# Twelve products of the identity with itself behind two of the prologue's weight transposes

## The chip, the cores and the metric

The kernel runs on one core of a Trainium2 chip. A core has five engines that work side by side, each on its own stream of instructions in order: TensorE (PE; its weight loads, PEld, are listed apart), VectorE (DVE), ScalarE (ACT), GpSimd (POOL) and SyncE (SP), which here only issues transfers. The metric is the device time of one execution in microseconds. TensorE's clock has two levels, 1.2 and 2.4 GHz; the profile gives the granted clock of a stretch as a share of the higher one.

## The reference

Attention with 8 heads over 8 batches of 576 tokens (head size 64), then a normalised feed-forward layer (512 to 2048 to 512) with a residual:

```python
scores = scale * np.matmul(q, k.transpose(0, 1, 3, 2))
mask_local = (rel >= 0) & (rel < 32)                       # heads 0 to 3
mask_strided = (rel >= 0) & (pos[None, :] % 32 == pos[:, None] % 32)   # heads 4 to 7
scores = np.where(masks, scores, -1e9)
attn = softmax(scores)                    # with 1e-9 added to the sum
x = np.matmul(attn, v)                    # heads side by side: 512 columns
xn = (x - mean(x)) / np.sqrt(var(x) + 1e-06) * g_ln
out = x + np.maximum(xn @ w_ch1, 0.0) @ w_ch2
```

All inputs and the output are float32.

## The kernel before

The 8 x 576 tokens are worked on as nine chunks of 512. The feed-forward weights lie in 16 blocks of 128 hidden columns, and each value is split into a high and a low part, so that a product is made of three. From about 45 us to the end TensorE runs these products almost without a gap, and the attention of later batches lies between them.

The **prologue** ahead of that (the first 45 us, and thinner until about 85 us) fills the pipeline. It prepares two batches of attention and the first eight weight blocks. Heads go in pairs: a, b, c, d are the four pairs of batch 0, and a1 to d1 those of batch 1. Pairs a and c are local, b and d strided; the names in the trace end in 0, 2, 1, 3 for a, b, c, d. The order of the prologue is written out by hand in the table `ORDER`, as steps with a letter and a pair (or a weight block):

- `L`: load; `R`: bring the two heads of a pair side by side (a copy `flat` by POOL or DVE, L371); `T`: nine transposes on TensorE (`t` and `tr`, L377); `C`: copies of the turned queries and keys (`qt`, `kt`, L388 to L396).
- `S`: scores (`sp`, L445 local, L457 strided); `M`: add the mask (`sm`, L472); `Z`, `U`, `E`: maximum, subtraction, exponential.
- `P`: transposes of the attention weights (`pp`, L498: five of 128 columns for a local pair, six for a strided one); `G`: ACT's copy of them (`pt`, L503); `V`: the product with the values (`av`, L514 or L523); `O`: divide by the sums (`xo`); `X`: transposes of the output (`px`, L559); `H`, `Y`: its high and low parts (`xh`, `xl`).
- `w0.cm` and the like: steps of weight block 0. `cm` (L270) is a float32 product 128 wide that gives a column mean.
- `F1`: the first products of the feed-forward layer, for chunk 0 (`ph`, L970).

Each engine takes its instructions in the order in which the steps were written; the end of the kernel ties every instruction to the one ahead of it on its engine. A step on TensorE that waits therefore holds up all later steps on TensorE. Loads are issued by SP in order too, and a rule in the loop over the steps lets each wait until earlier loads have landed, so that only so many are under way.

PSUM, into which TensorE writes, is shared out as banks. In the prologue the pool `ps_x` holds a working bank and two tiles, `s0` and `s1`, that the first products of the weight blocks 0 and 1 use (step `F1`, `product`). At its start the program runs four products of the identity with itself (`idle`, L922), 512 columns wide.

Of the kernel before, what the change touches and what calls it, by code (L numbers as in the profile page):

```python
# [8 lines left out]
F32 = mybir.dt.float32  # L9
# [10 lines left out]
ORDER = """  # L20
L.a L.b L.c R.a/DVE L.X0 T.a L.Y0 R.b/POOL C.ka/ACT C.qa/DVE L.X1 T.b R.c/POOL S.a L.d C.qb/DVE
C.kb/ACT M.a w0.sc0 T.c w0.lo0 Z.a/DVE S.b C.qc/ACT L.va w0.mg0 U.a C.kc/ACT w0.sg0 M.b S.c
w0.lo1 w0.bg w0.sc1 Z.b/DVE E.a w0.mg1 U.b w1.sc0 L.vb P.a w0.sg1 M.c R.d/POOL w1.lo0 E.b w1.mg0
w0.cs T.d G.a w1.sg0 P.b w1.bg C.qd/DVE C.kd/ACT L.Y1 L.vc G.b Z.c/DVE w0.cm S.d w0.ce U.c V.a
M.d L.X2 w0.hi0 w1.cs O.a E.c V.b L.Y2 w0.lw0 O.b w1.sc1 X.a w1.cm H.a L.a1 Z.d/DVE w1.lo1 X.b
D.c/POOL Y.a H.b w1.mg1 P.c L.vd Y.b G.c U.d w2.sc0 w1.sg1 w0.hi1 V.c w1.ce E.d w0.lw1 F1.0.b
O.c w2.lo0 P.d L.b1 w2.sc1 w2.mg0 R.a1/POOL G.d X.c w2.sg0 H.c T.a1 w2.lo1 w2.bg Y.c L.X3 w2.mg1
L.va1 C.ka1/ACT V.d w2.cs w2.sg1 F1.0.a C.qa1/ACT O.d w2.hi1 S.a1 L.Y3 w1.hi0 R.b1/POOL X.d M.a1
L.c1 w1.lw0 H.d Z.a1/DVE T.b1 w3.lo0 U.a1 Y.d F1.1.b w3.sc0 F1.1.a C.qb1/ACT C.kb1/DVE D.a1/POOL
# [17 lines left out]
def kernel(  # L47
# [10 lines left out]
    nc = tc.nc  # L58

    B, H, S, D = q.shape  # L60
    DM, DFF = w1.shape
    P = 128
# [9 lines left out]
    CH = 512  # L72
# [25 lines left out]
    ps_x = sums_ctx.enter_context(  # L98
        tc.tile_pool(name="ps_x", bufs=1, space=bass.MemoryType.PSUM, side="right"))
# [11 lines left out]
    ident = keep.tile([P, P], F32, name="ident")  # L111
# [731 lines left out]
    def ffn2(run, f, h, tiles):  # L843
        for i in tiles:
            products(run.po[i], f, h, i, slice(0, DM), f == run.f0, f == run.f1 - 1)
# [135 lines left out]
    def second(n, half):  # L981
        if n == "0" and not half:
            sums_late()
            runs[0].open()
            banks[:] = [(ps_a, "a")]
        x = hidden[int(n)]
        ffn2(runs[0], int(n), (x["h"], x["l"]), range(2 * half, 2 * half + 2))

    weights = {"sc": Split.scaled, "lo": Split.low, "mg": Split.magnitude, "sg": Split.sign,
               "bg": Split.by_g, "cs": Split.chunks_sum, "cm": Split.column_mean,  # L990
               "ce": Split.centred, "hi": Split.high, "lw": Split.rest}
# [8 lines left out]
        "V": lambda x: named[x].v_values(), "O": lambda x: named[x].v_scale(),  # L1000
        "St": lambda x: named[x].x_store(), "X": lambda x: named[x].x_rows(),
        "H": lambda x: named[x].x_high(), "Y": lambda x: named[x].x_low(),
        "F1": product, "hh": high, "hl": low,
        "F2a": lambda n: second(n, 0), "F2b": lambda n: second(n, 1)}
    FLIGHT = 45
    queued = []
# [12 lines left out]
    for step in ORDER.split():  # L1019
        what, x = step.split(".", 1)  # L1020
        n0 = len(tc.nc.cur_bb.bb.instructions)
        if what[0] == "w":
            i = x[2:]
# [3 lines left out]
        for ins in tc.nc.cur_bb.bb.instructions[n0:]:  # L1027
            if "DMA" not in type(ins).__name__:
                continue
            n, behind = len(queued), 0  # L1030
# [396 lines left out]
    for i, x in enumerate(residuals):  # L1427
        po = fresh_bank(f"po{B}_{i}")
        n = NFC if i + 1 < NT else NFC - 2
# [54 lines left out]
```

## Time and profile before

| what | value |
|---|---|
| three timed runs | 895.68, 898.46, 900.03 us; median 898.46 us |
| the profiled execution | 896.8 us, of it the span of the profile 895.0 us |
| TensorE busy | 878.1 us, 98% of the span |
| DVE, ACT, POOL busy | 455.5, 242.2, 238.7 us |
| mean granted clock | 0.994 |
| TensorE busy in the first 45 us | 33.49 us |

Times within the profile count from the span's start. "Idle" is the time in which an engine ran nothing just ahead of an instruction, and the profile names what ended it. A "record" is what TensorE shows of an instruction: a float32 product makes two, a transpose one.

### The profile page before, as it was taken

To read this page: it belongs to the slowest core of one execution; us is meant where nothing else is said; L and a number is where in the kernel's file an instruction comes from. 1 tells how busy PE (TensorE), PEld (TensorE's weight loads), DVE (VectorE), ACT (ScalarE), POOL (GpSimd) and SP (SyncE) were. 2 spreads that over 40 slices of the span, in tenths; PEclk is the share of its full clock that TensorE was granted. 3 is DMA by queue.
4 is the path that set the end of the run, shared out by engine and by line. 5 is a ranking of instruction groups with operands and counts; after the bars stand their busy time and mean duration, and the time that the engine had idled before them with its cause. 6 is when DMAs were issued, how large, how long until landed. Compare 5 with 4: busy or idle time off the path is not lost.

```text
span 895.0 us, 18342 instructions
## 1 busy us (share of the span) xinstructions
PE 878.1 (98%) x7431; PEld 721.1 (81%) x7431; DVE 455.5 (51%) x855; ACT 242.2 (27%) x433; POOL 238.7 (27%) x293
## 2 busy tenths in 40 slices
PE   6899999999999999999999999999999999999998
PEld 4678888888888888888888888888888788888886
DVE  5797475446745455544645455455652764232400
ACT  4666465112211111111111111112122443333200
POOL 6678187110100010000100000001000468676000
PEclk9899999999999999999999999999999999999999
DMA  9999881117786655756585759596942001001210
GB/s 210 205 212 254 199 259 36 21 46 176 149 166 117 119 106 107 143 113 117 97 150 103 133 96 171 107 134 130 167 109 79 13 13 47 1 0 44 91 32 23
DMA packets 330972, 100.64 MB, mean 112 GB/s; under 512 B 269712, under 2 KB 321800, under 8 KB 330888
## 3 DMA queue, kind: packets, MB, share of 16 engines
q1 hardware_dynamic: 259320, 86.41, 43.7%
q10 hardware_dynamic: 71568, 13.07, 9.8%
q8 instruction: 58, 0.95, 0.5%
q14 instruction: 26, 0.21, 0.1%
HBM read 72.37 MB, written 27.06 MB: 111 GB/s over the span
## 4 chain that ended last, share of the span: by engine, by line
PE 95%; ACT 1%; DVE 1%; DMA 1%; issue 1%; SPq 0%; POOL 0%; POOLq 0%; ACTq 0%
PE po L840 44%; PE ph L815 33%; PE u L1250 5%; PE sv L659 5%; PE v L1250 2%; PE c L1250 1%; PE px L690 1%; DMA rows<-in_k_dram 1%; PE pp L498 1%; PE av L514 0%; PE cm L270 0%; PE t L377 0%; PE ph L970 0%; PE px L559 0%; PE sp L457 0%
## 5 line engine op out<-in xcount | busy, mean ns | idle before, releaser
L840 PE MATMUL po<-w,hh 128*128 128x512 f32 x1024 | 320.4, 394 | 0.0
L815 PE MATMUL ph<-xh,w 128*128 128x512 f32 x880 | 290.4, 391 | 0.0
L840 PEld LDWEIGHTS po<-w,hh 128*128 128x128 f32 x1024 | 188.9, 188 | 39.3
L826 DVE SCALAR_TENSOR_TENSOR hl<-ph,hh 128x512 fp32r<-128x512 f32 x112 | 77.4, 691 | 268.9 <-ACT hh L821 268.9
L840 PE MATMUL po<-w,hl 128*128 128x512 f32 x512 | 199.4, 390 | 0.0
L815 PEld LDWEIGHTS ph<-xh,w 128*128 128x128 f32 x880 | 165.2, 188 | 34.2
L815 PE MATMUL ph<-xl,w 128*128 128x512 f32 x440 | 171.2, 389 | 0.0
L821 ACT ACTIVATE hh<-ph 128x512 fp32r<-128x512 f32 x112 | 66.9, 597 | 339.8 <-PE ph L815 258.7
L488 POOL TENSOR_TENSOR sm<-sm,mx 128x640 f32<-128x640 f32 (+1 forms) x32 | 40.6, 1269 | 344.9 <-issue 201.1
L840 PEld LDWEIGHTS po<-w,hl 128*128 128x128 f32 x512 | 96.1, 188 | 20.5
L815 PEld LDWEIGHTS ph<-xl,w 128*128 128x128 f32 x440 | 82.7, 188 | 16.8
L493 ACT ACTIVATE sm<-sm 128x640 f32<-128x640 f32 (+1 forms) x32 | 23.8, 742 | 104.3 <-POOL sm L488 104.3
L782 POOL TENSOR_TENSOR rs<-rs,mhalf 128x1 f32<-128x1 f32 x28 | 15.4, 551 | 121.3 <-DVE rs L781 93.1
L840 PE MATMUL po<-w,h 128*128 128x512 f32 x186 | 42.3, 389 | 0.0
L1117 POOL TENSOR_TENSOR sr<-sr,w 128x256 f32<-128x256 f32 x48 | 40.2, 837 | 3.8
L840 PEld LDWEIGHTS po<-w,h 128*128 128x128 f32 x186 | 34.9, 188 | 7.2
L1117 POOL TENSOR_TENSOR s<-sr,s 128x256 fp32r<-128x256 f32 x32 | 24.7, 803 | 25.5 <-ACT s L1236 25.5
L239 DVE SCALAR_TENSOR_TENSOR p<-s,p 128x512 uint32<-128x512 uint32 x32 | 22.0, 688 | 11.4 <-ACT p L235 11.2
L484 DVE TENSOR_REDUCE mx<-sm 128x10 f32<-128x640 f32 (+1 forms) x32 | 26.3, 822 | 1.9
L1117 DVE TENSOR_TENSOR x<-po,x 128x512 f32<-128x512 f32 x8 | 5.3, 688 | 39.6 <-PE po L840 29.9
L671 DVE TENSOR_TENSOR xo<-sv,den 128x256 f32<-128x256 f32 (+1 forms) x72 | 24.0, 389 | 0.0
L1117 DVE TENSOR_TENSOR p<-u,p 128x512 f32<-128x512 f32 x8 | 5.5, 692 | 34.1 <-PE u L1250 34.1
(193 smaller groups left out, 995.6 us busy)
## 6 DMA issues: line engine op xcount, KB each, us to landing
s<-in_moe_w_ch_dram SPq DMA_DIRECT2D x32, 512.0 KB
out_dram<-x SPq DMA_DIRECT2D x32, 256.0 KB
raw<-in_q_dram SPq DMA_DIRECT2D x104, 72.0 KB
raw<-in_k_dram ACTq DMA_DIRECT2D x68, 72.0 KB
x<-xdl SPq DMA_DIRECT2D x34, 128.0 KB
x<-xds SPq DMA_DIRECT2D x34, 128.0 KB
xdl<-xo SPq DMA_DIRECT2D x16, 256.0 KB
wd<-sm SPq DMA_DIRECT2D x10, 384.0 KB
```

The lines of the kernel that those rows point to most:

```text
L239: nc.vector.scalar_tensor_tensor(out=self.p[i], in0=self.bits(i), scalar=3, in1=self.p[i], op0=ALU.logical_shift_left, op1=ALU.bitwise_or)
L484: engine(self.mx[:, :, 0:nt], self.smv, axis=AX.X)
L488: nc.gpsimd.tensor_tensor(out=sm, in0=sm, in1=mx[:, :, 0:nt].unsqueeze(3).broadcast_to([P, 2, nt, w]), op=ALU.subtract)
L493: nc.scalar.activation(out=self.smv, in_=self.smv, func=AF.Exp, scale=SCALE)
L659: nc.tensor.matmul(dst, at, by, start=True, stop=True, tile_position=pos)
L671: nc.vector.tensor_tensor(out=xot[0:n, :, t0:t1], in0=src, in1=pv.den[0:n, :, t0:t1].unsqueeze(3).broadcast_to([n, 2, t1 - t0, D]), op=ALU ...
L815: nc.tensor.matmul(ph, w[:, cc], x[:, cc, :], start=(n + k == 0), stop=(n == NCC - 1 and k == 2))
L821: nc.scalar.activation(out=hh, in_=ph, func=AF.Relu)
L826: nc.vector.scalar_tensor_tensor(out=hl, in0=ph, scalar=0.0, in1=hh.bitcast(F32), op0=ALU.max, op1=ALU.subtract)
L840: nc.tensor.matmul(po, hx[:, cs], w, start=(start and n == 0), stop=(stop and n == 2))
L1117: engine.tensor_tensor(out=out, in0=a, in1=b, op=op)
L1250: nc.tensor.matmul(po, a[:, c], b[:, c, :], start=(start and c + k == 0), stop=(stop and c == 1 and k == 2), skip_group_check=True)
```

## The change

A new kind of step, `K`, stands in the table twice: `K.8` right behind `P.a`, and `K.4` right behind `P.c`. It multiplies the 128 x 128 identity by itself in float32, eight and four times, into the first 128 columns of a PSUM tile with the tag `s1`. Nothing reads the result, and the tile's place is used by `F1` later.

```diff
-w0.lo1 w0.bg w0.sc1 Z.b/DVE E.a w0.mg1 U.b w1.sc0 L.vb P.a w0.sg1 M.c R.d/POOL w1.lo0 E.b w1.mg0
+w0.lo1 w0.bg w0.sc1 Z.b/DVE E.a w0.mg1 U.b w1.sc0 L.vb P.a K.8 w0.sg1 M.c R.d/POOL w1.lo0 E.b w1.mg0
...
-D.c/POOL Y.a H.b w1.mg1 P.c L.vd Y.b G.c U.d w2.sc0 w1.sg1 w0.hi1 V.c w1.ce E.d w0.lw1 F1.0.b
+D.c/POOL Y.a H.b w1.mg1 P.c K.4 L.vd Y.b G.c U.d w2.sc0 w1.sg1 w0.hi1 V.c w1.ce E.d w0.lw1 F1.0.b
...
+    def beats(n):
+        t = ps_x.tile([P, CH], F32, tag="s1", name=f"beats{n}")[:, 0:P]
+        for i in range(int(n)):
+            nc.tensor.matmul(t, ident, ident, start=True, stop=True)
...
-        "F1": product, "hh": high, "hl": low,
+        "K": beats, "F1": product, "hh": high, "hl": low,
```

On TensorE the first place reads as follows before the change, from pair c's scores (`sp_1`) over pair a's weight transposes (`pp_0`) and pair d's transposes (`t_3`, `tr_3`) to pair d's scores (`sp_3`); the numbers behind are those of the tiles:

```order
L445 MATMUL sp_1_381<-kt_l,qt_l 32x64 x36
L498 MATMUL pp_0_435<-ident,sm_200 128x128 x5
L377 MATMUL t_3_454<-ident,flat_3_446 128x128 x8
L377 MATMUL tr_3_455<-ident,flat_3_446 128x128
L498 MATMUL pp_2_469<-ident,sm_199 128x128 x6
L270 MATMUL cm_490<-r_0_377,mean 128x128
L457 MATMUL sp_3_492<-kt_s,qt_s 64x54 x22
```

And after it, in the same place on TensorE:

```order
L445 MATMUL sp_1_381<-kt_l,qt_l 32x64 x36
L498 MATMUL pp_0_435<-ident,sm_200 128x128 x5
L992 MATMUL beats_441<-ident 128x128 x8
L377 MATMUL t_3_463<-ident,flat_3_455 128x128 x8
L377 MATMUL tr_3_464<-ident,flat_3_455 128x128
L498 MATMUL pp_2_478<-ident,sm_199 128x128 x6
L270 MATMUL cm_499<-r_0_377,mean 128x128
L457 MATMUL sp_3_501<-kt_s,qt_s 64x54 x22
```

Eight products stand between pair a's weight transposes and pair d's transposes; the rest is in its old order, with other tile numbers.

The second place on TensorE before the change, from the second column mean over pair c's weight transposes (`pp_1`) and its product with the values (`av_1`) to the first products of weight block 0:

```order
L270 MATMUL cm_611<-r_1_467,mean 128x128
L559 MATMUL px_2_623<-ident,xo_2_603 128x128 x6
L498 MATMUL pp_1_636<-ident,sm_200 128x128 x5
L514 MATMUL av_1_658<-v_l_188,pt_1_650 32x65 x40
L970 MATMUL ph_0_702<-xh_613,w_0_562 128x512
```

And after it:

```order
L270 MATMUL cm_620<-r_1_476,mean 128x128
L559 MATMUL px_2_632<-ident,xo_2_612 128x128 x6
L498 MATMUL pp_1_645<-ident,sm_200 128x128 x5
L992 MATMUL beats_651<-ident 128x128 x4
L514 MATMUL av_1_672<-v_l_188,pt_1_664 32x65 x40
L970 MATMUL ph_0_716<-xh_622,w_0_571 128x512
```

Four products stand between pair c's weight transposes and its product with the values. The other engines and SP's loads keep their order throughout. The added products wait for nothing but their turn on TensorE.

## Rows read from the trace of the kernel before

**Rows 1.** The page: TensorE's granted clock in tenths, 40 equal slices.

```profile
PEclk9899999999999999999999999999999999999999
```

**Rows 2.** Stretches (us): busy time and instructions by engine, clock, DMA share, GB/s.

```profile
17.50:20.00 2.50, 0.94 (x6) 0.63 (x6) 2.46 (x6) 1.96 (x4) 1.47 (x2) 0.97 1.04 180
20.00:25.00 5.00, 3.76 (x16) 3.39 (x17) 2.47 (x5) 1.89 (x5) 3.37 (x5) 0.50 1.01 182
25.00:27.50 2.50, 2.50 (x116) 2.22 (x116) 1.19 (x2) 1.52 (x4) 2.42 (x4) 0.66 1.31 196
27.50:30.00 2.50, 2.04 (x88) 1.79 (x70) 2.31 (x8) 0.62 (x2) 2.38 (x3) 1.00 1.10 315
30.00:32.50 2.50, 1.62 (x13) 1.18 (x12) 2.48 (x4) 2.07 (x4) 1.80 (x2) 1.00 1.01 244
32.50:35.00 2.50, 1.29 (x81) 1.12 (x80) 2.30 (x4) 2.43 (x6) 0.64 (x2) 0.71 0.66 131
35.00:37.50 2.50, 2.50 (x32) 1.93 (x16) 2.00 (x5) 1.28 (x3) 1.97 (x2) 0.61 0.61 147
45.00:100.00 55.00, 54.28 (x646) 43.90 (x645) 40.50 (x70) 32.40 (x57) 36.52 (x36) 1.00 0.90 214
```

**Rows 3.** Timeline of TensorE: start, duration (us), instruction, records [idle before, releaser].

```profile
17.94 0.77 PE L498 MATMUL pp<-ident,sm 128*128 128x128 f32 x5
21.01 1.97 PE L377 MATMUL t<-ident,flat 128*128 128x128 f32 x8 [2.31 <-DVE r L245]
...
24.70 0.77 PE L270 MATMUL cm<-r,mean 128*128 128x128 f32 x2 [0.23 <-ACT kt_s L396]
25.40 1.49 PE L457 MATMUL sp<-kt_s,qt_s 64*64 64x54 f32 x44
...
29.83 0.39 PE L270 MATMUL cm<-r,mean 128*128 128x128 f32 x2
30.69 0.84 PE L559 MATMUL px<-ident,xo 128*128 128x128 f32 x6 [0.48 <-DVE xo L539]
31.93 0.77 PE L498 MATMUL pp<-ident,sm 128*128 128x128 f32 x5 [0.40 <-DVE xl L604]
33.91 1.41 PE L514 MATMUL av<-v_l,pt 64*32 64x65 f32 x80 [1.21 <-ACT pt L503]
```

**Rows 4.** Timeline of TensorE's weight loads at the program's start.

```profile
3.23 0.34 PEld L922 LDWEIGHTS idle<-ident 128*128 128x128 f32 x1 [0.52 <-issue]
```

**Rows 5.** Timeline of TensorE where the granted clock is 1.00.

```profile
14.14 0.91 PE L457 MATMUL sp<-kt_s,qt_s 64*64 64x54 f32 x44
...
43.63 1.06 PE L377 MATMUL t<-ident,flat 128*128 128x128 f32 x8 [0.26 <-DVE sm L478]
...
47.05 1.26 PE L457 MATMUL sp<-kt_s,qt_s 64*64 64x54 f32 x44 [0.17 <-DVE kt_s L396]
...
50.06 1.04 PE L514 MATMUL av<-v_l,pt 64*32 64x65 f32 x80
```

**Rows 6.** Chain of work that ended last: start, duration (us), what.

```profile
35.32 1.58 PE ph L970 x3
...
40.78 0.89 PE ph L970 x3
```

**Rows 7.** Timelines of POOL, DVE and ACT, around the two places.

```profile
19.81 1.14 POOL L371 COPY flat<-rows 128x1152 f32<-128x1152 f32 x1 [1.01 <-DMA rows<-in_k_dram]
...
20.27 0.69 DVE L245 SCALAR_TENSOR_TENSOR r<-s,p 128x512 uint32<-128x512 uint32 x1
...
32.70 1.11 DVE L604 TENSOR_TENSOR xl<-px,xh 128x480 fp32r<-128x480 f32 x2 [0.22 <-ACT xh L599]
...
24.27 0.28 ACT L396 COPY kt_s<-tr 128x64 f32<-128x64 f32 x1
```

**Rows 8.** POOL's copy of b1; SP's waits from 26 to 42 us (total, times, longest).

```profile
41.84 1.15 POOL L371 COPY flat<-rows 128x1152 f32<-128x1152 f32 x1 [1.37 <-DMA rows<-in_k_dram]
...
SPq L419 <- DMA s<-in_moe_w_ch_dram: 2.9, 2, 2.3
```

## The prediction

> **What bounds the kernel now.** I read the clock line of the page first [rows 1]: TensorE is granted its full clock in every slice of 22 us but the second (about 22 to 45 us), which shows 8 tenths. The program is bound by TensorE (878.1 us of the 895.0 us span are busy, the table above), so what can be won at all is idle time or slow time in the prologue. The stretch table places it [rows 2]: the mean clock is 0.97 from 17.5 to 20 us, 0.50 from 20 to 25 us, 0.66 from 25 to 27.5 us, 1.00 until 32.5 us, then 0.71 and 0.61. There are only two levels, 1.2 and 2.4 GHz, so 0.97 means that half clock began 0.15 us before 20 us, and 0.66 that it ended 1.7 us after 25 us: about 19.85 to 26.7 us. The second spell is 1.45 us of one stretch and 1.95 us of the next: 33.55 to 36.95 us. That is 10.2 us at half clock, and since half clock can cost no more than half of the time spent in it, 5.1 us is the ceiling of everything that this change can win by the clock: 0.57% of 896.8 us.
>
> What came before each fall: from 17.5 to 20 us TensorE was busy 0.94 of 2.50 us, from 30 to 32.5 us 1.62 of 2.50 us. From 27.5 to 30 us it was busy 2.04 us and the clock stayed [rows 2]. The timeline shows the two holes [rows 3]: the first pair's weight transposes end at 18.71 us and the next work, pair d's transposes, starts at 21.01 us; the third pair's end at 32.70 us and the next, its values product, starts at 33.91 us. The change puts work into just these two holes.
>
> **Part 1, the eight products behind the first pair.** Price: a float32 product 128 wide makes two records on TensorE. The nearest row is the column mean (same shape and type): 0.39 us a product at full clock, 0.77 us at half [rows 3]. That includes the end of the pipe, so eight of them cost at most 3.1 us at full clock. For a stream I take the four products at the program's start: their records are 512 wide and the weight loads start 0.86 us apart (0.34 us busy behind 0.52 us of idle time) [rows 4]. A quarter of the width is 0.21 us a record. I read this as the pace at half clock, though the page's first slice shows 9 tenths or more [rows 1], since eight transposes 128 wide take 1.06 us at full clock and 1.97 us at half, some 0.11 and 0.21 us apart once the last one's end is off [rows 3, 5]. So 16 records take 15 x 0.107 + 0.28 for the last (0.39 less 0.107) = 1.9 us at full clock, 3.4 to 3.7 us at half. I take 1.9 us. They start behind the fifth transpose, at about 18.5 us, and end at 20.4 us (21.6 us by the column mean's price).
>
> Is that hidden? The queue behind them holds pair d's transposes. These wait for POOL's copy, which ends at 20.95 us, and start at 21.01 us; the row names a DVE operation that ends at 20.96 us [rows 3, 7]. So there is 0.55 us of cover; by the upper price the delay is 0.6 us. The destination is a PSUM tile that nobody reads, and the order shows no wait on the products, so no other engine gets a new wait.
>
> What they change: TensorE is busy from 17.8 to 20.4 us instead of 18.7. From 17.5 to 20 us it is then busy for 0.94 + 1.29 = 2.2 us, much as in the stretch from 27.5 us (2.04 us), behind which the clock stayed [rows 2]. I take it that the clock holds here too. Then pair d's transposes take 1.06 us instead of 1.97 (0.91 less), the column mean 0.39 instead of 0.77 (0.38 less), and the strided scores 0.91 instead of 1.49 (0.58 less) [rows 3, 5]. Pair b's six transposes between are covered by the wait for ACT's copy that ends at 24.55 us [rows 3, 7]; that copy follows pair d's transposes through DVE, so it comes 0.91 us earlier. Sum: 1.87 us earlier at the first values product. The DVE chain from there to 32 us follows TensorE step by step, so I carry 1.87 us on to the third pair.
>
> A page speaks on the rest of this stretch. Of the 1.62 us before the second fall nearly all was transposes (six of pair b's output, 0.84 us, five of pair c's weights, 0.77 us) [rows 2, 3], and yet the clock fell. The Trainium skill, "TensorE: Matmul & The Clock Gate", section "Part 4: PE-mode transpose", says that transposes do not count as busy time for the clock; this trace agrees at that fall. By that rule real products, as here, are the right filler, but the transposes of pairs d and b behind them hold nothing; what that would give is the second rival.
>
> **Part 2, the four products behind the third pair.** Eight records: 7 x 0.107 + 0.28 = 1.0 us at full clock, 1.6 us by the single price, 1.9 us at half. They start about 32.5 us and end at 33.5 us. The values product behind them starts at 33.91 us because it needs the ACT copy and a PSUM bank that DVE reads until 33.81 us [rows 3, 7]: 0.4 us of cover, and a delay of 0.2 to 0.5 us by the other prices. If the second spell goes, the values product takes 1.04 instead of 1.41 us (0.37) [rows 3, 5], and the three products behind it 0.89 instead of 1.58 us on the chain (0.69) [rows 6]: 1.06 us. Both parts together: 2.93 us at most.
>
> **What is late next.** This does not all arrive. Pair b1's transposes start at 43.63 us [rows 5]. They need POOL's copy of b1's rows, which starts at 41.84 us after 1.37 us of waiting for a load, and lasts 1.15 us [rows 8]: it ends at 42.99 us. SP issues that load in order behind the values' loads, whose waits are for other loads (2.9 us, the longest 2.3 us) [rows 8], not for TensorE. So it will land where it did, and with 0.05 us to react the transposes cannot start before 43.05 us: 0.58 us earlier, not 2.93. TensorE works in order, so everything behind them waits too. After that 0.17 us of idle time is left to win, at the scores of 47.05 us, which wait for DVE's copy of the same transposes [rows 5]; from 45 us on TensorE is busy 54.28 of 55 us [rows 2]. Sum: 0.58 + 0.17 = 0.75 us. The ends: 0.2 us, if the upper prices of both parts eat the gain before the load, and 1.2 us, if the load lands half a microsecond earlier.
>
> The profiled execution took 896.8 us (span 895.0); the sum on it is 896.05 us. The three timed runs are 895.68, 898.46 and 900.03 us, so it lies below their median; the mean of all four is 897.74 us, and I set the cases against that: 897.74 - 0.75 = **897.0 us**.
>
> **The rivals.**
> - The full gain arrives: the load of b1 lands earlier in most executions, and 2.93 us come through: 894.8 us. For it: nothing in one trace says how far a load's landing moves from run to run. Against it: in this trace POOL waits 1.37 us for it [rows 8].
> - The clock falls later, not less: the 15 transposes of pairs d and b follow the eight products and the clock drops behind them. Then 0.91 us of part 1 stays, but two values products run at half clock (0.37 us each), and 0.17 us is left; if the second spell stays as well, that is all: 897.6 us. For it: 1.62 us of transposes did not hold the clock from 30 us [rows 2].
> - Slower: the added products run at half clock. If the clock has fallen by 18.5 us instead of 19.85 us, the eight end at about 22.0 us and hold up pair d by 1.0 us; the four end 0.4 us after the values product could start. All of it is on TensorE's path: 1.4 us, 899.1 us. It decides from a fall 1.35 us earlier than here. Against it: the clock is 0.97 in the whole stretch [rows 2].
> - The change does nothing: identity products leave the clock as it is and are hidden: 897.7 us.
>
> **How the numbers follow.** Forecast 0.50, full gain 0.16, later fall 0.16, slower 0.12, nothing 0.06. The four times shown differ by 4.35 us with the same code, so a median of three moves by a good microsecond either way. From 894.0 (the full gain, with 0.7 us of that) to 899.6 us (the slower case with 0.5 us) I leave out about 2 in 10. Half a per cent, 4.5 us, is about what a measurement of this kernel can tell from no change: faster means under 893.97, slower over 902.95. Only the full gain with a low run reaches the first (0.05), and only the slower case with two high runs the second (0.03).
>
> **What the profile after would show.** Right: clock 1.00 from 17.5 to 27.5 us and from 32.5 to 37.5 us; the products done by 20.4 and near 32 us; pair d's transposes in about 1.06 us; POOL's copy of b1 still near 41.8 us, after a longer wait, with TensorE idle in front of b1's transposes, which start near 43.05 us. Wrong: a copy of b1 that starts well before 41 us (full gain); half clock between 22 and 30 us (later fall); products 0.21 us apart with pair d's transposes behind 21.5 us (slower). A change of over 4 us in either direction would show that something outside the prologue moved.

## The result and the profile after

The changed kernel takes 901.55 us (median of 11 runs, 899.17 to 906.36), the kernel before 897.3 us in the same comparison (11 runs, 895.68 to 900.03). The ratio is 1.0051, with a 95% interval from 1.0031 to 1.0070: slower by 2.8 to 6.3 us, and outside the range that was forecast. (A ratio here is that of the whole comparison, not the quotient of the two medians.) The profiled execution of the changed kernel is one of its faster ones, 899.44 us with a span of 897.7 us: 2.7 us over that of before.

The clock row of the page after, TensorE's granted clock in 40 slices, has lost the 8 of [rows 1]:

```profile
PEclk9999999999999999999999999999999999999999
```

The table of stretches shows the prologue in more detail (us; busy time and instructions of TensorE, its weight loads, DVE, ACT and POOL; granted clock, share of the DMA engines, GB/s). It answers to [rows 2]:

```profile
20.00:22.50 2.50, 2.50 (x26) 2.50 (x25) 2.03 (x6) 0.58 (x2) 2.42 (x4) 1.00 0.87 131
35.00:37.50 2.50, 0.71 (x6) 0.45 (x5) 2.24 (x4) 1.96 (x4) 1.22 (x2) 1.00 0.65 129
37.50:40.00 2.50, 2.50 (x45) 2.17 (x48) 0.94 (x2) 1.05 (x3) 2.10 (x3) 0.62 0.82 213
40.00:45.00 5.00, 4.74 (x115) 3.84 (x110) 3.32 (x8) 2.61 (x7) 2.54 (x3) 0.85 1.02 268
```

Both half-clock spells of before are gone. A new one follows a stretch in which TensorE was busy throughout before [rows 2]: from 35 to 37.5 us it is busy for 0.71 us only, and then the clock is 0.62 and 0.85. TensorE's timeline (start, duration, operation, records, idle time before and what ended it) shows the products and the new pause. It answers to [rows 3, 5]:

```profile
18.73 0.24 PE L445 MATMUL sp<-kt_l,qt_l 64*32 64x64 f32 x1 [2.31 <-issue]
18.90 0.77 PE L498 MATMUL pp<-ident,sm 128*128 128x128 f32 x5
19.51 1.95 PE L992 MATMUL beats<-ident 128*128 128x128 f32 x16
21.29 1.04 PE L377 MATMUL t<-ident,flat 128*128 128x128 f32 x8
...
24.45 0.91 PE L457 MATMUL sp<-kt_s,qt_s 64*64 64x54 f32 x44
25.28 1.04 PE L514 MATMUL av<-v_l,pt 64*32 64x65 f32 x80
...
31.04 1.06 PE L992 MATMUL beats<-ident 128*128 128x128 f32 x8
32.46 1.08 PE L514 MATMUL av<-v_l,pt 64*32 64x65 f32 x80 [0.37 <-issue]
...
37.48 1.44 PE L377 MATMUL t<-ident,flat 128*128 128x128 f32 x8 [1.79 <-POOL flat L371]
...
47.34 0.91 PE L457 MATMUL sp<-kt_s,qt_s 64*64 64x54 f32 x44 [0.18 <-DVE kt_s L396]
```

Up to 35 us this is the forecast, though the first products start 1 us late: 1.95 and 1.06 us of products, the transposes and scores behind them at full clock. Then TensorE is early for pair a1's rows, waits 1.79 us for POOL's copy of them, and is at the scores of 47.34 us no earlier than before (47.05 us).

To follow the time further I took the starts of the 112 `hh` activations (L821), one for each block of the main loop, and subtracted those of before. At 69 us the changed kernel is 0.54 us ahead, and from there to the end of the main loop TensorE hardly pauses, so lead or lag moves only where it does: -0.31 us at 280, +0.29 at 470, +0.68 at 607, +0.73 at 644, then **+3.58 us at 649 and +2.64 us from 655 us to the end**. So 3.2 us are lost behind the prologue, 1.9 us of them at one place. The other 1.3 us are hardly the change's: against this one execution of before, the kernels below with products and the turns of before (e1, e5, e6, e7) lose 1.0 to 1.2 us there too. At the one place ScalarE's timeline reads, before:

```profile
643.99 4.97 ACTq L419 DMA_DIRECT2D v_s<-in_v_dram  x6
649.41 0.60 ACT L821 ACTIVATE hh<-ph 128x512 fp32r<-128x512 f32 x1 [4.84 <-DMA v_s<-in_v_dram]
```

and after (ACTq is ScalarE's queue issuing transfers, here the six loads of the short values `v_s`):

```profile
644.72 8.17 ACTq L419 DMA_DIRECT2D v_s<-in_v_dram  x6
652.99 0.60 ACT L821 ACTIVATE hh<-ph 128x512 fp32r<-128x512 f32 x1 [7.70 <-DMA v_s<-in_v_dram]
```

The six issues take 8.17 us in place of 4.97, the next `hh` stands behind them in ScalarE's order, and TensorE waits for the `hl` that follows from it. From TensorE's timeline of after:

```profile
654.37 0.50 PE L815 MATMUL ph<-xh,w 128*128 128x512 f32 x1 [1.61 <-DVE hl L826]
```

The chain of work that ended last, after, says what the six issues waited for (start, duration, what):

```profile
642.23 4.19 DMA xds<-xo
...
646.44 2.03 DMA v_s<-in_v_dram
...
648.66 0.49 SPq L722
...
649.20 2.97 DMA sp<-wd
...
652.19 0.28 ACTq L419
...
652.51 0.38 ACTq L419
...
652.99 0.61 ACT hh L821
```

A store of SP, a load of ScalarE, a load of SP (`sp<-wd`), and only then ScalarE's last two loads: the two queues wait for each other in turn, though the data have nothing to do with each other.

The built programs say why. The 790 transfers of SP (632) and ScalarE (158) share eight counting semaphores in turn, and each waits until the transfer eight turns ahead of it has landed. Which transfer gets which turn is not in the table of steps; the build works it out for the program as a whole, presumably from the times that it expects (no run here shows how). Both engines issue the same transfers in the same order before and after, but the two orders are merged differently at eleven places, all behind turn 254. At the last one:

```
v_s load of ScalarE      1st   2nd   3rd   4th   5th   6th
before, its turn         701   702   704   706   708   710
  waits for              693   694   696   698   700   702
after, its turn          703   706   708   710   712   714
  waits for              695   698   700   702   704   706
turns 690 to 693 stores of the result, 694 to 697 loads of x, 698 and 699 stores xds, 700 store wd,
sp loads of SP: 703, 705, 707, 709 before; 701, 702, 704, 705 after (issued once 698, 699, 700 have landed)
```

Before, the 4th and 5th load wait for stores, none for an `sp` load. After, the 4th and 5th (turns 710 and 712) wait for `sp` loads, which SP can only issue once the stores have landed. As built, the eight products alone give the same altered turns as the change; the four alone leave all 790 as before.

### The profile page after: what moved, and what is told of

Same layout as the page of the kernel before. It is cut to its first block, busy times and chain, and to the rows that moved or that the text cites. A ratio compares the mean times of both kernels' runs of the same rounds, so it can differ in the third digit from the quotient of the medians.

```text
span 897.7 us, 18388 instructions
## 1 busy us (share of the span) xinstructions
PE 880.0 (98%) x7455; PEld 722.3 (80%) x7455; DVE 455.2 (51%) x855; ACT 241.5 (27%) x433; POOL 238.7 (27%) x293
## 5 line engine op out<-in xcount | busy, mean ns | idle before, releaser
L821 ACT ACTIVATE hh<-ph 128x512 fp32r<-128x512 f32 x112 | 66.8, 596 | 343.2 <-PE ph L815 243.2
```

Source lines behind the costliest of these rows:

```text
L821: nc.scalar.activation(out=hh, in_=ph, func=AF.Relu)
```

## The experiments

The theory, **T**: the altered turns cost the time, not the products. The first rival, **R**: the products cost it. Both can be separated by holding the turns. The hold is a block at the end of the program, which chains the transfers of both queues in the order that a string gives (S17: seventeen transfers of SP, A1: one of ScalarE). It costs no instruction; held in its own turns, the kernel before is built exactly as without it.

```diff
         last[ins.engine] = ins.name
+    turns = "A1 S254 A1 S1 ... S11 A2 S1 A1 S1 A1 S1 A1 S1 A1 S69 ..."
+    lines = {"S": [], "A": []}
+    for ins in tc.nc.cur_bb.bb.instructions:
+        if "DMA" in type(ins).__name__:
+            lines["S" if "SP" in str(ins.engine) else "A"].append(ins)
+    before = None
+    for run in turns.split():
+        for _ in range(int(run[1:])):
+            ins = lines[run[0]].pop(0)
+            if before is not None:
+                tc.add_manual_dep(ins, before, ...)
+            before = ins.name
```

Each comparison has its own runs of the kernel before; their median is 897.16 us in the first group (e1 to e4), 898.13 us in the second (e5 to e8) and 897.46 us in the third (e9 to e12). So ratios are compared, not times across groups.

**e1: all products, the turns of before.** The edit is that block in the changed kernel.

> The changed kernel with all twelve products, but with the 790 transfers of SP's and ScalarE's queues held in the turns that they had before the change (the transfers share eight semaphores in turn, and each waits until the one eight turns earlier has landed). Theory T (the loss comes from the altered turns alone): the lead of about 0.5 us won in the prologue is kept to the end, so 0.3 to 1.0 us under the kernel before, 896.3 to 897.0 us; hh at 649 us is no longer 3.6 us late, and TensorE's wait of 1.61 us for hl near 654 us is gone. Rival R (the products themselves cost it, by the clock or by the matmuls' state on the chip): as the changed kernel, 900 to 902 us.

898.84 us, ratio 1.0018 (1.0007 to 1.0030). The wait near 654 us is gone, the six loads issue in 4.05 us and `hh` follows on time:

```profile
645.96 4.05 ACTq L419 DMA_DIRECT2D v_s<-in_v_dram  x6
651.38 0.60 ACT L821 ACTIVATE hh<-ph 128x512 fp32r<-128x512 f32 x1 [4.84 <-PE ph L815]
```

Two thirds of the loss go with the turns, but the lead of 0.5 us does not appear: this execution is 0.87 us late at 69 us already. T holds for the larger part; its gain from the prologue, and with it the 896.3 to 897.0 us, was wrong.

**e2: no products, the turns of the changed kernel**, and **e3: no products, the altered turns at the last place alone.** The string is the changed kernel's as a whole, or in this one piece:

```diff
-S11 A2 S1 A1 S1 A1 S1 A1 S1 A1 S69
+S13 A1 S2 A1 S1 A1 S1 A1 S1 A1 S1 A1 S65
```

> The kernel before, without any added product, with its transfers in the turns that the changed kernel has. Theory T: the loss without the gain, 3 to 5 us over the kernel before, 900.5 to 902.5 us, with a TensorE wait of 1 to 2 us for hl near 655 us. Rival R (the products cost it): no change, 897 to 898 us.

> The kernel before with only the last of the altered places taken over from the changed kernel: the six loads of v_s that ScalarE issues near 644 us have the turns 703, 706, 708, 710, 712, 714 in place of 701, 702, 704, 706, 708, 710. Theory T, if this place carries the loss: 1.5 to 3 us over the kernel before, 899 to 900.5 us, hh near 649 us 2 to 4 us late. If the loss is spread over all the places: under 1 us, 897.3 to 898.3 us. Rival R: no change.

e2: 903.09 us, 1.0068 (1.0051 to 1.0085). e3: 901.55 us, 1.0048 (1.0034 to 1.0062). So the turns alone, with not one product in the program, make the kernel as slow as the change does, and the last place alone does most of it. ScalarE's timelines, e2 first, then e3:

```profile
645.00 10.08 ACTq L419 DMA_DIRECT2D v_s<-in_v_dram  x6
655.18 0.60 ACT L821 ACTIVATE hh<-ph 128x512 fp32r<-128x512 f32 x1 [10.19 <-DMA v_s<-in_v_dram]
```

```profile
643.99 9.09 ACTq L419 DMA_DIRECT2D v_s<-in_v_dram  x6
653.18 0.60 ACT L821 ACTIVATE hh<-ph 128x512 fp32r<-128x512 f32 x1 [8.62 <-DMA v_s<-in_v_dram]
```

In e3 `hh` is level with the kernel before at 644 us (643.96 against 643.97) and 3.77 us late at the next. The medians of e3 and e2 lie 1 and 0.6 us above what was expected.

What makes e2 the slower of the two shows in its trace at the same place. TensorE waits 4.10 us for `hl` there, longer than in e3 (2.53 us) and the changed kernel (1.61 us), and behind that wait its granted clock is 0.50, the lower of its two levels, until about 661.7 us; in the two others it stays 1.00. The first line is TensorE's timeline, the others are stretches (TensorE's busy time, granted clock, share of the DMA engines, GB/s):

```profile
656.56 0.79 PE L815 MATMUL ph<-xh,w 128*128 128x512 f32 x1 [4.10 <-DVE hl L826]
...
655.00:657.50 2.50, 0.94 (x2) 0.50 0.44 119
657.50:660.00 2.50, 2.50 (x7) 0.50 0.23 69
660.00:662.50 2.50, 2.50 (x71) 0.67 0.14 48
```

So e2 goes from 0.42 us late at 644 us to 7.17 us late at 655 us, and only 0.4 of the 4.35 us that it is then behind e3 had arisen before. Whether the slower executions of the changed kernel and of e3 lost more in this way too, no trace shows.

**e4: all products, the changed turns, but the last place as before.**

> The changed kernel with all twelve products and with its transfers in its own turns, except that the last altered place (the six loads of v_s near 644 us) has the turns of the kernel before. Theory T, if this place carries the loss: 1.5 to 3 us under the changed kernel, 898.5 to 900 us; hh near 649 us at most 1 us late. If the loss is spread: 900.5 to 901.5 us. Rival R: as the changed kernel, 901.5 us.

899.09 us, 1.0019 (1.0004 to 1.0034): as e1, and 0.32% below the change's ratio. The ten other places thus cost nothing that can be told: 0.25 us between the medians of e1 and e4. One expectation was missed: `hh` is 2.58 us late near 649 us in this execution, not at most 1 us; but 2.49 us of that were there at 644 us already, ahead of the last place. Rival R is out for the larger part of the loss, from both sides: the turns do it without the products (e2, e3), and the products don't do it without the turns (e1, e4).

What is left is the prologue: 0.75 us were forecast as won, and e1 and e4 lie 0.2% over the kernel before. A second theory, **L**: loads set the prologue's end, so neither the clock nor the products matter to it. Its rivals: **P**, the products' time lies on the path; **G**, the clock's gain arrives in part.

**e5: the four products alone; e6: the eight alone; e7: sixteen and eight**, all in the turns of before.

```diff
-... P.a K.8 w0.sg1 ...        -... P.a K.8 ...  P.c K.4 ...
+... P.a w0.sg1 ...   (e5)     +... P.a K.16 ... P.c K.8 ...   (e7)
```

> Only the four products behind the third pair's weight transposes (the eight at the first pair left out); the transfers keep the turns that they had before without being held. Theory L (the loads of the weight rows s, for which ScalarE waits until about 54 us, set the end of the prologue, and neither the clock nor the products' time moves it): within 1 us of the kernel before, 896.5 to 898.0 us. Rival P (the products' own time lies on the path and the clock gives nothing back): their 1.06 us less 0.4 us of cover, 897.8 to 898.3 us. Rival G (the clock's gain arrives in part): 0.3 to 1 us under the kernel before.

> Only the eight products behind the first pair's weight transposes (the four at the third pair left out), with the transfers held in the turns of the kernel before. Theory L: within 1 us of the kernel before, 896.5 to 898.2 us. Rival P: their 1.95 us less 0.55 us of cover, 898.3 to 898.8 us. Rival G: 0.5 to 1.9 us under the kernel before.

> Sixteen and eight products in place of eight and four, with the transfers held in the turns of the kernel before: 24 more records of about 0.107 us, 2.6 us more work on TensorE than in the run with eight and four in the same turns (898.84 us). Theory L: most of it disappears in the waits for loads that follow, under 1 us more, 898.3 to 899.8 us. Rival P: the whole of it, 901 to 901.7 us.

e5: 897.86 us, 0.9991 (0.9980 to 1.0001). e6: 898.93 us, 1.0009 (0.9996 to 1.0022). e7: 897.89 us, 0.9996 (0.9986 to 1.0007). e6 lies above the ranges of both L and P, e7 below both. But twice the products, 3.74 and 1.95 us of them in the profile, cost nothing that can be measured, where P asked for over 901 us: P is out, at this limit on loads. The mean clock of e7's twelve executions is 0.998 to 1.000, that of the 35 of the kernel before beside them 0.991 to 0.998, and e7 is not faster either: G has nothing to show. (Among all 95 executions of the kernel before in the three groups, the 14 with a mean clock of 0.992 or less took 899.39 us on average, the 19 with 0.997 or more 897.05 us. A pause of TensorE, as in e2, can do both, lengthen the time and lower the clock; which came first there is not shown.) ScalarE's timeline says who waits instead (L229 and L235 read the weight rows `s` that SP has loaded). e5, then e7:

```profile
55.72 0.67 ACT L229 ACTIVATE s<-s 128x512 f32<-128x512 f32 x1 [2.22 <-DMA s<-in_moe_w_ch_dram]
```

```profile
45.33 0.62 ACT L235 ACTIVATE p<-s 128x512 uint32<-128x512 uint8 x1 [2.11 <-DMA s<-in_moe_w_ch_dram]
```

Where TensorE is early, it or ScalarE mostly waits for a load; the first `hh` then follows the L229 of about 55 us by 0.6 us, or TensorE waits for pair b1's scores behind the L235 of 45 us (2.28 us in e7).

**e8: no products, ScalarE's loads in consecutive turns** at four places, the last of them:

```diff
-S11 A2 S1 A1 S1 A1 S1 A1 S1 A1 S69
+S11 A6 S73
```

> The kernel before without any added product; the turns of its transfers changed at four places (near 386, 478, 600 and 644 us) so that the six v_s loads or four raw loads that ScalarE issues in one go stand in consecutive turns, and none of them waits for a transfer that SP issues between them. If a load of ScalarE that waits for SP's newest transfers is what delays hh (theory T): the six loads near 644 us issue in about 3 us in place of 4.97 us, hh is never later than in the kernel before, and the time is 0 to 1.5 us under it, 895.5 to 897.2 us. Rival: SP's loads of sp behind them wait in turn, 897.5 to 900 us.

897.58 us, 0.9995 (0.9982 to 1.0008). The six loads, which took 4.97 us before, issue in 2.63 us:

```profile
644.89 2.63 ACTq L419 DMA_DIRECT2D v_s<-in_v_dram  x6
650.31 0.60 ACT L821 ACTIVATE hh<-ph 128x512 fp32r<-128x512 f32 x1 [4.84 <-PE ph L815]
```

The mechanism is confirmed a third time, now in the other direction, and it brings no time: before, `hh` was just not late at this place, so there was nothing to win but room. (Elsewhere `hh` was up to 1.35 us late in this execution, at 511 us, and the median lies 0.4 us above the range; those parts of the expectation were missed.)

**e9: all products in these gathered turns.**

> The changed kernel with all twelve products, its transfers in the gathered turns of the run e8 (the loads that ScalarE issues in one go stand in consecutive turns). Theory T and L together (the loss is the turns, and the products bring nothing): as the kernel before, within 1.2 us of it; hh near 649 us not late and the six loads near 644 us issued in under 3.5 us. Rival P (the products cost 1 to 2 us by themselves): 1 to 2 us over the kernel before.

897.65 us, 1.0011 (0.9995 to 1.0027). This is the change with its loss repaired: the six loads take 2.61 us, and the kernel can't be told from that before. So it is neither faster nor slower, and no version here beats the kernel before.

**e10 to e12: the loads of the prologue moved directly**, by the limit on loads in flight (`FLIGHT`, 45 before), in the turns of before:

```diff
-    FLIGHT = 45
+    FLIGHT = 60     (e10 without products, e11 with all twelve; 36 in e12, without)
```

> The kernel before, without products, in its own turns, with the limit on loads in flight in the prologue at 60 in place of 45, so that SP issues each load earlier. Theory L (the loads set the end of the prologue): if they wait for each other, 0.5 to 2 us faster; if the transfers' rate is full already, within 0.5 us. Rival C (TensorE's clock and work set it): no change.

> All twelve products, the turns of the kernel before, and the limit on loads in flight at 60. Theory L: the same as the run without products and with the limit at 60, within 0.8 us; if the loads no longer bind, the clock's gain of up to 1.5 us appears as the difference of the two. Rival P: 1 to 2 us slower than that run.

> The kernel before, without products, in its own turns, with the limit on loads in flight in the prologue at 36 in place of 45, so that SP issues each load later and nothing else is altered. Theory L: ScalarE waits longer for the rows of s near 45 to 60 us, hh is 1 to 3 us later at 69 us and the time is 1 to 3 us over the kernel before. Rival C (TensorE's clock and work set the end of the prologue): within 0.5 us.

e12: 898.18 us, 1.0015 (1.0003 to 1.0028), 0.78 us late at 69 us, with ScalarE's L229 at 56.04 us after a wait of 1.76 us for `s`: the sign that L asked for, but less than its 1 to 3 us. e10 went the other way than expected: 902.22 us, 1.0038 (1.0019 to 1.0057), seven of nine executions from 901.18 to 903.0 us and two at 896.6 and 896.86 us. The profiled one, of the seven, is 5.1 us late at 69 us. Its rows of TensorE's timeline:

```profile
20.16 0.31 PE L445 MATMUL sp<-kt_l,qt_l 64*32 64x64 f32 x1 [3.69 <-issue]
...
33.07 0.65 PE L514 MATMUL av<-v_l,pt 64*32 64x65 f32 x21 [4.72 <-issue]
```

TensorE stood twice for nothing that the profile shows as a wait. e11 is slower still, 1.0072 (1.0047 to 1.0097), eleven of its twelve executions scattered from 896.57 to 908.79 us with a median of 905.6 us. That is some 3 us over e10, where L expected the same within 0.8 us and P 1 to 2 us more, so at this limit P is not ruled out, though the two intervals overlap. Its profiled execution is one of the two quick ones (897.49 us): 1.43 us ahead at 69 us, with a stall of 2.54 us at L445 and only 0.36 us at L514. So more clock can come through if the loads come earlier and no such stall occurs, but one execution does not show how often. What happened in the slow ones no trace shows.

So with the limit on loads the prologue's end moved in the profiles, 0.78 us later (e12), 5.1 us later (e10) and 1.43 us earlier (e11), where 2.6 us more products moved nothing at the limit of 45. But the 5.1 us are a stall that names no load. L is the reading that fits best; that loads alone set the prologue's end is not shown, nor which ones: in the changed kernel it was a1's rows, in e7 and e1 the `s` of 45 us, in e3, e5 and e8 the `s` of 55 us.

## Where the prediction was right and where it went wrong

- **What the products do on TensorE: right.** 1.95 and 1.06 us in the trace, 1.9 and 1.0 by the sum. They started at 19.51 instead of 18.5 us, since the last score product ahead of them stood 2.31 us, 1.07 us longer than before; that was no effect of the products, as e2 without any has 2.29 us there.
- **The clock holds behind them: right in the changed kernel**, wrong as a rule. In e4 and e11 the eight products themselves ran at half clock, 3.33 and 3.55 us, the slower case of the prediction, and pair d's transposes came at 22.92 and 23.24 us. TensorE had stood 2.32 and 2.54 us at L445 ahead of that; but in the changed kernel, at full clock, it had stood 2.31 us. The transposes behind the products did not make the clock fall in the changed kernel, so its second rival (later fall) was wrong there. The Trainium skill's rule on transposes ("TensorE: Matmul & The Clock Gate", "Part 4: PE-mode transpose") stood behind that rival; here transposes alone, from 21.29 us on, and 0.96 us of idle time followed the products, and the granted clock stayed 1.00 up to 37.5 us, so the fall that the rival drew from the rule did not come here.
- **The second spell at half clock: read as fixed, but it is not.** Part 2 priced its removal at 1.06 us. Without any product it stands before and in e2 (the third pair's values product takes 1.41 us), but not in e3, e8 and e12 (1.03 us), with the same instructions on TensorE. So that the transposes made it fall in the one trace is not borne out, and four products could win back that time only in some executions. In e12's stretches (columns as in e2's) TensorE is as busy as in [rows 2], and the clock stays:

```profile
30.00:32.50 2.50, 1.62 (x14) 1.00 0.85 272
32.50:35.00 2.50, 1.29 (x84) 1.00 0.63 154
```

- **What is late next: the wrong load, and one too few.** The sum went from the third pair straight to pair b1's rows. In between stand a1's transposes, which had waited for ScalarE until 38.62 us before; with TensorE 2.4 us earlier there they waited 1.79 us for a1's rows, and behind that pause the clock fell again. b1's transposes then started at 43.91 us, not near 43.05 us, and not behind POOL's copy of b1, which had started early, at 41.31 us: they waited for DVE, as the row of before has it too [rows 5]. The term was 0.75 us. In single profiles the kernels with products and the limit of 45 stand at 69 us at -0.54 (the change), +0.87, +0.32, +0.45, +1.34, +0.06 and +0.71 us (e1, e4, e5, e6, e7, e9) against the kernel before; those without at -0.47, -0.59 and -0.71 (e2, e3, e8). The gain is not there; if anything the prologue is later by some tenths of a microsecond to one. The timed ratios of the five runs with products and harmless turns lie from 0.9991 to 1.0018. Whether products lag a little, and why, stays open.
- **No other engine gets a new wait: this step failed, and with it the forecast.** It was argued from the order of instructions on each engine, which in fact did not change. But the transfers' waits depend on how two engines' orders are merged, and that is settled by the build for the program as a whole. The products moved them at eleven places, from turn 255 on, of which the last cost 4.3 us by itself (e3). The prediction named the sign ("A change of over 4 us in either direction would show that something outside the prologue moved") but gave it no mechanism, and the range ended at 899.6 us.
- **The slower rival** was put at 899.1 us by products at half clock. The sign came true by another mechanism, one that doesn't need the products to run.

## What to carry to other kernels

A change that adds no wait of its own can still move others' waits: where transfers of several engines share semaphores in turn, compare each transfer's wait in the built programs, not only the order on each engine, and keep the loads that a compute engine issues in one go in consecutive turns, ahead of transfers that wait for stores; here that took the loss away (e9) and by itself won nothing (e8). Before paying for the clock in a stretch, list every load that the stretch waits for: the time won reaches only as far as the next one.

## What the runs showed of the hardware beyond that

TensorE's stall named "issue" at L445, where no edit altered TensorE's order, was 0.30 us in e3, 1.24 us before, 2.31 us after and 3.69 us in e10. The DMA answer lists a queue of the kind "instruction" (packets, MB, share of the DMA engines' time). Its packet of this stretch lies between 15 and 16 us before, first row, and between 17 and 18 us in e10, second row; the stall ended at 17.77 and 20.16 us:

```profile
q8 instruction: 1, 0.02, 7.2%
```

```profile
q8 instruction: 1, 0.02, 8.3%
```

In e3, with the shortest stall, it lies between 14 and 15 us. That fits instructions that arrive late behind the loads. But the stall was 2.46 us in e12 too, with fewer loads in flight, and at the limit of 45 it scattered from 0.30 to 2.32 us, so the number of loads does not settle it; no run here tested it apart, and it stays a reading.
